# Attention with a decaying state, then a gated FFN: q's columns read as even tokens and then odd ones, and a new order for every engine

## The chip, the core and the metric

The kernel runs on one core of a Trainium2 chip. Five engines work side by side, each through its own list of instructions in order: PE (TensorE, the matmuls), ACT (ScalarE), DVE (VectorE), POOL (GpSimd) and SP (SyncE, which here only issues DMAs). The metric is the device time of one execution in microseconds. Profiles are of one execution each; times are medians of several.

## The reference

```python
f = 1.0 / (1.0 + np.exp(-f_logit))                  # q, k, v, f_logit: (4, 8, 768, 48)
for t in range(S):
    state = f[:, :, t, :, None] * state + np.einsum('bhd,bhe->bhde', k[:, :, t], v[:, :, t])
    y[:, :, t] = np.einsum('bhd,bhde->bhe', q[:, :, t], state)
x = y.transpose(0, 2, 1, 3).reshape(B * S, H * D)   # (3072, 384)
out = (np.maximum(x @ w_gate, 0.0) * (x @ w_val)) @ w_out     # d_ff 1536, float32 out
```

## The kernel before

**Attention by chunks.** Each of the four batches' 768 tokens are cut into chunks of 128. For a chunk the kernel sums the logarithms of the gates over the tokens (a matmul with a triangle), takes exponentials of the sums, scales k and q with them ("hats"), and turns both over, so that tokens lie along the columns (`qkT`). The scores of a chunk are then a matmul of the two, a mask and a matmul with v; what comes from earlier chunks is a product of q with a 48 x 48 state per head (two heads share a tile). The chunk's own k and v then bring the state forward.

**Steps and units.** The work has six steps, c = 0 to 5, each of four slots, b = 0 to 3. In steps 2 to 5 a slot is one chunk of one batch. In steps 0 and 1 two slots form a unit: a unit takes 256 neighbouring tokens of one batch, two chunks, loaded so that a partition holds a pair of neighbouring tokens. The even tokens of the pairs make one slot, the odd ones the other. A unit's keys thus lie in an order of their own, but the outputs must come out as tokens 0, 1, 2 and so on, so the score matmul reads q's columns in the order of the tokens: one column from the even tile, one from the odd tile, 64 of each, the two tiles 2 KB apart in a partition. That is `turned` (line 626); the units' scores use it (line 645) and so does their product with the state (line 703). `tmask` (lines 345 to 352) is the units' mask. Each unit's output y is copied from PSUM into `xT` (`out_way`, line 606).

**The FFN.** The 512 tokens of a step make 12 blocks of hidden columns, each of three matmuls into a gate bank (g), three into a value bank (u) (line 787), a relu on ACT or DVE (r, lines 792 and 793), and a product on DVE (p, line 795). In step 0 the first four blocks are done in two halves of 256 tokens. Then for each slot three times four matmuls with w_out (o, line 808), a copy out of PSUM (d) and a store (S).

**Names.** An operation is named by a letter, the step and the slot. L: load (f, k, q or v; the load f5.2 serves slots 2 and 3 of step 5). ef, ln: the two ACT passes over f. cum: the sum over tokens. ek, eq: exponentials. dc: decay. hk, hq: hats. tk, tq: transposes on PE (steps 0 and 1), ck, cq their copies. xh: the transposes by DMA that take their place in steps 2 to 5, on SP's queue. v: copy of v. s: scores, m: mask. y: product with v, yi: a unit's product with the state. kv, ss, sd, st: the state. x or n: copy of y; xx: the transpose by DMA into `xT` (steps 2 to 5, SP's queue). So s02 is the scores of the unit in slots 2 and 3 of step 0, g20.3 is the gate of hidden block 3 of step 2, o21.4 the second third of slot 1's output in step 2. wg, wv, wo with two numbers are loads of weights by POOL (first block + how many).

**What sets the order.** The lists `ORDER` (line 23) are written out: for each engine the operations by number, in the order in which it does them; which engine does an elementwise operation follows from the list that it stands in. A number `~25512` in PE's list stands for 25 matmuls of 512 columns on zeros (fillers, line 872), which keep PE at work. `BANKS` deals PSUM's eight banks to the operations that open one. `HELD` (line 80) makes some loads wait for the landing of another. The waits between engines follow from what an operation reads and writes. A planner outside the kernel finds the lists; it uses the costs that stand with the operations, for instance 0.01765 us for a DMA packet of a unit's load. They do nothing on the chip.

**Where an operation stands in the trace.** Engines work through their lists in order, so counting along a list gives each recorded instruction its name, and each DMA its time of landing.

## Time and profile before

| | us |
|---|---|
| runs shown | 199.95, 202.79, 202.70 |
| median | 202.7 |
| the profiled execution | 200.93 |
| its span, first to last instruction | 199.2 |
| mean granted TensorE clock | 1.000 |
| PE busy | 187.6 (94%) |
| DVE busy | 135.2 (68%) |
| ACT busy | 92.2 (46%) |
| POOL busy | 62.4 (31%) |
| HBM read and written | 25.95 and 4.72 MB |

The slices of the page cut the span into 40 equal parts of about 5 us; a digit is the busy share in tenths. The chain of waits lists in order of time what the end of the kernel hung on. In the timelines, "PE L787 ... x11 [1.53 <-DMA xT<-xn]" means eleven matmuls of that line in a row, before which PE stood idle for 1.53 us until a DMA into `xT` had landed. "SPq" is the time in which SP's queue issues a DMA: it grows when earlier transfers are not yet through.

### The profile page before, as it was taken

Reading aid. Unit: us, or ns where it says so; the run is one execution under the profiler, and the core shown is the slowest. Engines: PE = TensorE matmul, PEld = TensorE weight load, DVE = VectorE, ACT = ScalarE, POOL = GpSimd, SP = SyncE. Lnnn points to the kernel's source line nnn. Section 1 sums busy time; section 2 is a strip of 40 time slices with the busy share of each in tenths; the row PEclk is TensorE's granted clock in tenths of the full one; section 3 lists DMA queues with packets and bytes.
Section 4 is the critical chain, followed back from the end, with each engine's and each line's share of the span. In section 5 each row is a group of like instructions: output and inputs, shape, how many; then the busy total and the mean of one; then the engine's idle time right before and its main releaser. Section 6 shows DMA issues by size and latency. Waiting matters only on the chain.

```text
span 199.2 us, 4503 instructions
## 1 busy us (share of the span) xinstructions
PE 187.6 (94%) x1818; PEld 108.9 (55%) x1837; DVE 135.2 (68%) x248; ACT 92.2 (46%) x198; POOL 62.4 (31%) x93
## 2 busy tenths in 40 slices
PE   7969989999999999969999979999979999999994
PEld 2436657557565546744457644565654465455563
DVE  4179747767875979751899779687644785246841
ACT  2777744126368649831322694822166420331220
POOL 8488970041017565320612466330003000000000
PEclk9999999999999999999999999999999999999999
DMA  6999899999972999988999849996945201011103
GB/s 153 325 325 205 121 172 210 232 282 242 222 178 62 241 208 219 218 181 215 240 212 204 165 105 264 225 190 113 229 137 158 53 7 36 0 42 69 50 36 122
DMA packets 113636, 33.19 MB, mean 167 GB/s; under 512 B 106832, under 2 KB 113360, under 8 KB 113616
## 3 DMA queue, kind: packets, MB, share of 16 engines
q1 hardware_dynamic: 98432, 25.83, 57.1%
q0 software_dynamic: 3776, 3.54, 11.5%
q10 hardware_dynamic: 11408, 3.54, 7.3%
q8 instruction: 14, 0.23, 0.5%
q14 instruction: 6, 0.05, 0.1%
HBM read 25.95 MB, written 4.72 MB: 154 GB/s over the span
## 4 chain that ended last, share of the span: by engine, by line
PE 66%; DMA 10%; SPq 10%; DVE 6%; ACT 3%; ACTq 3%; issue 2%; DVEq 0%
PE ps L787 33%; PE ps L808 19%; SPq L411 6%; DMA k_in<-in_k_dram 5%; DMA f_in<-in_f_logit_dram 3%; SPq L560 3%; DVE hats L541 3%; ACTq L406 3%; PE ps L584 2%; PE ps L645 2%; PE ps L667 2%; PE ps L503 1%; PE ps L552 1%; DVE ptm L652 1%; DMA xT<-xn 1%
## 5 line engine op out<-in xcount | busy, mean ns | idle before, releaser
L795 DVE TENSOR_TENSOR gT<-relu,ps 128x512 bf16<-128x512 bf16 (+1 forms) x76 | 48.2, 656 | 21.0 <-PE ps L787 12.8
L792 ACT ACTIVATE relu<-ps 128x512 bf16<-128x512 f32 (+1 forms) x50 | 28.4, 575 | 58.7 <-PE ps L787 34.5
L787 PE MATMUL ps<-xT,wg 128*128 128x512 bf16 (+1 forms) x222 | 52.4, 368 | 2.8 <-DMA xT<-xn 2.6
L787 PE MATMUL ps<-xT,wv 128*128 128x512 bf16 (+1 forms) x218 | 52.1, 368 | 0.6
L808 PE MATMUL ps<-wo,gT 128*128 128x384 bf16 (+2 forms) x300 | 52.3, 320 | 0.0
L808 PEld LDWEIGHTS ps<-wo,gT 128*128 128x128 bf16 x300 | 27.5, 97 | 17.9 <-issue 0.5
L787 PEld LDWEIGHTS ps<-xT,wg 128*128 128x128 bf16 x228 | 23.7, 108 | 23.0 <-DMA xT<-xn 2.6
L787 PEld LDWEIGHTS ps<-xT,wv 128*128 128x128 bf16 x228 | 23.5, 108 | 18.9
L540 POOL TENSOR_TENSOR hats<-q_in,expo 128x384 bf16<-128x384 f32 x15 | 15.9, 1070 | 41.2 <-ACT expo L518 29.0
L540 POOL TENSOR_TENSOR hats<-k_in,expo 128x384 bf16<-128x384 f32 x17 | 17.5, 1036 | 16.7 <-DMA k_in<-in_k_dram 12.3
L793 DVE TENSOR_SCALAR relu<-ps 128x512 bf16<-128x512 f32 (+1 forms) x26 | 16.8, 656 | 8.3 <-PE ps L787 7.9
L592 DVE TENSOR_TENSOR ptm<-ps,tri 128x512 bf16<-128x512 f32 x32 | 20.3, 683 | 2.1 <-PE ps L584 2.1
L814 ACT ACTIVATE osb<-ps 128x384 f32<-128x384 f32 (+1 forms) x15 | 7.1, 480 | 17.7 <-PE ps L808 16.5
L456 POOL TENSOR_TENSOR st<-ssum,dec 128x384 bf16<-128x384 f32 x11 | 9.6, 880 | 16.8 <-DVE ssum L454 16.8
L478 ACT ACTIVATE f_in<-f_in 128x768 f32<-128x768 f32 x12 | 10.0, 841 | 8.4 <-issue 4.4
L516 ACT ACTIVATE expo<-ps 128x384 f32<-128x384 f32 x24 | 11.6, 495 | 1.9 <-PE ps L506 1.6
L518 ACT ACTIVATE expo<-ps 128x384 f32<-128x384 f32 x24 | 11.5, 491 | 2.3 <-DVE hats L541 1.4
L652 DVE TENSOR_TENSOR ptm<-ps,tmask 128x512 bf16<-128x512 f32 x16 | 10.3, 682 | 3.2 <-PE ps L645 3.2
L872 PE MATMUL ps<-zeros 128*128 128x512 bf16 x37 | 11.4, 452 | 0.6 <-DVE ptm L652 0.4
L481 ACT ACTIVATE bneg<-f_in 128x768 bf16<-128x768 f32 x12 | 10.0, 844 | 0.2
L815 DVE COPY osb<-ps 128x384 f32<-128x384 f32 (+1 forms) x10 | 5.3, 526 | 7.0 <-PE ps L808 7.0
L570 POOL CAST vpad<-v_in 128x384 bf16<-128x384 f32 x10 | 5.1, 518 | 15.2 <-DMA v_in<-in_v_dram 13.0
(74 smaller groups left out, 168.1 us busy)
## 6 DMA issues: line engine op xcount, KB each, us to landing
out_dram<-osb SPq DMA_DIRECT2D x23, 192.0 KB, 2.2
f_in<-in_f_logit_dram SPq DMA_DIRECT2D x11, 384.0 KB, 5.8
v_in<-in_v_dram SPq DMA_DIRECT2D x10, 384.0 KB, 6.1
q_in<-in_q_dram SPq DMA_DIRECT2D x9, 384.0 KB, 5.7
k_in<-in_k_dram SPq DMA_DIRECT2D x9, 384.0 KB, 4.8
k_in<-in_k_dram ACTq DMA_DIRECT2D x3, 384.0 KB, 7.3
q_in<-in_q_dram ACTq DMA_DIRECT2D x3, 384.0 KB, 6.0
v_in<-in_v_dram ACTq DMA_DIRECT2D x2, 384.0 KB, 6.7
```

The costliest lines, as they stand in the source:

```text
L411: op = add("L" + item, {**by("SP", lambda: sy.dma_start(dst, src), (0.42, 0.42)), **by("ACT", lambda: sc.dma_start(dst, src), (0.5, 0.5))} ...
L516: add(f"ek{c}{b}", by("ACT", lambda: sc.activation(ex[:, 1, :], bc.ap[:, 0:HD], AF.Exp, scale=1.0), act_(HD)), [bc], [f"expk{ei}"], key=P + 1)
L518: add(f"eq{c}{b}", by("ACT", lambda: sc.activation(ex[:, 0, :], bc.ap[:, 0:HD], AF.Exp, scale=-1.0), act_(HD)), [bc], [f"expq{ei}"], key=P ...
L540: return {**by("POOL", lambda: gp.tensor_tensor(o, i_, e_, ALU.mult), pool_(HD)), **by("DVE", lambda: ve.tensor_tensor(o, i_, e_, ALU.mult ...
L592: add(f"m{c}{b}{j}", by("DVE", lambda b=b, j=j, mi=mi: ve.tensor_tensor(ptm[mi][:, j, :, :], s[b, j].ap[:, :].rearrange("p (n t) -> p n t" ...
L652: add(f"m{c}{b2[i]}{j}", by("DVE", lambda i=i, j=j, mask=mask: ve.tensor_tensor(ptm[mi[i]][:, j, :, :], s[j, i].ap[:, :].rearrange("p (n t ...
L787: z = te.matmul(bank.ap[:, 0:n], wt[:, kt, w_cols(j)], xT[xi][:, kt, n0:n1], start=(kt == 0), stop=(kt == NK - 1))
L792: add(f"r{c}{b0}.{j}", {**by("ACT", lambda: sc.activation(rdst, gate.ap[:, 0:n], AF.Relu), act_(n)), **by("DVE", lambda: ve.tensor_scalar_ ...
L793: **by("DVE", lambda: ve.tensor_scalar_max(rdst, gate.ap[:, 0:n], 0.0), dve_(n))}, [gate], [f"relu{ri}"], key=P)
L795: add(f"p{c}{b0}.{j}", by("DVE", lambda: ve.tensor_tensor(gT[gi][:, j, n0:n1], rdst, val.ap[:, 0:n], ALU.mult), dve_(n)), [val, f"relu{ri} ...
L808: z = te.matmul(o.ap[:, 0:e1 - e0], gT[gi][:, j, b * C:(b + 1) * C], wo[:, j, e0:e1], start=(j == 0), stop=(j == NJ - 1))
L872: te.matmul((op.opens[0].ap if op.opens else banks[7])[:, 0:fill % 1000], zeros[:, 0:128], zeros[:, 0:fill % 1000], start=True, stop=True, ...
```

## The change

Four edits, and the lists.

1. `turned` gives the 64 even columns first, then the 64 odd ones, each in one run. The scores and the state product of the units so come out with their columns as (even, odd).
2. The masks `tmask` and `tlow` of the units are made in that order of columns: the same selections, with a pattern of two dimensions.
3. The copies x00 to x13 of the units' outputs write every other column of `xT`, so that tokens stand in order again.
4. Three costs for the planner are other numbers (loads 0.0193 and 0.0130 a packet, not 0.01765 and 0.0118; 0.64 us for a unit's product with v).
5. `ORDER`, `HELD` and `BANKS` are new. No operation is added or removed. 117 elementwise operations and loads change their engine: 38 from ACT to DVE and 28 back, 22 from POOL to DVE and 14 back, 7 loads from ACT's queue to SP's and 4 back (Lq0.2, Lv1.0, Lk2.0, Lv2.2), 4 others between ACT and POOL. Those that leave ACT's queue are Lq0.0, Lf0.2, Lq1.0, Lk1.2, Lq1.2, Lk4.2 and Lv5.0. Fillers are 42, not 40, with 22 instead of 25 at the start.

```diff
@@ masks
-            select(f"tmask{i}", tmask[i][:], -17, compare_op=ALU.is_ge, fill=0.0, base=-i, pattern=[[1, 128]], channel_multiplier=-2)
+            select(f"tmask{i}", tmask[i][:].rearrange("p (x m) -> p x m", x=2), -17, compare_op=ALU.is_ge, fill=0.0, base=-i, pattern=[[1, 2], [2, 64]], channel_multiplier=-2)
...
@@ out_way
         if X_WAY[w] == "t":
-            add(f"x{c}{b}", copies(xdst, lambda: y.ap[:, 0:HD].rearrange("p (n t) -> p n t", n=NK), HD), [y], x_key, key=P + 8)
+            xsrc = lambda: y.ap[:, 0:HD].rearrange("p (n t) -> p n t", n=NK)
+            if w < 2 * UNITS:
+
+                xdst = xdst.rearrange("p n (m i) -> p n i m", i=2)
+                xsrc = lambda: y.ap[:, 0:HD].rearrange("p (n i m) -> p n i m", n=NK, i=2)
+            add(f"x{c}{b}", copies(xdst, xsrc, HD), [y], x_key, key=P + 8)
...
@@ turned
-        return bass.AP(tensor=at.tensor, offset=at.offset, ap=[list(at.ap[0]), [1, 64], [2 * NP * C, 2]])
+        return bass.AP(tensor=at.tensor, offset=at.offset, ap=[list(at.ap[0]), [2 * NP * C, 2], [1, 64]])
```

The lists by name, cut to what the prediction speaks of (before, then after):

```
SP  before  Lf0.0 Lv0.2 Lq0.2 Lf1.0 Lk0.2 Lf1.2 Lk1.0 Lq2.2 ...
SP  after   Lf0.0 Lq0.0 Lf0.2 Lv0.2 Lk0.2 Lf1.2 Lf1.0 Lq1.2 Lq1.0 Lk1.0 Lk1.2 Lv1.2 Lf2.0 Lv2.0 Lf2.2 S00 S02
            Lq2.2 Lq2.0 Lk2.2 Lf3.0 Lq3.0 xh21 xh20 Lk3.0 xh23 xh22 S01 S03 xh31 xx20 xh30 xx21 Lv3.0 Lf3.2
            xx22 S10 xx23 Lk3.2 Lq3.2 Lv3.2 S12 S13 xx31 xh33 xh32 S11 xx30 Lq4.0 Lf4.0 Lk4.0 Lf4.2 ...
SP  before  ... Lk5.0 Lv5.2 xh42 xh43 xh51 xh50 xx41 xx40 Lk5.2 Lq5.2 Lf5.2 xx43 xx42 S32 ...
SP  after   ... Lf5.0 Lk5.0 Lk5.2 Lq5.0 xx41 xx40 Lf5.2 Lv5.0 xh51 xh50 xx42 xx43 S23 S30 Lq5.2 Lv5.2 ...
ACT before  Lf0.2 Lk0.0 Lq0.0 Lv0.0 ef00 ef02 ln00 ln02 eq01 ek01 ek00 ...
ACT after   Lv0.0 Lk0.0 Lq0.2 ef00 ln00 eq00 ek01 dc00 ek00 eq01 ef02 ck00 ln02 ck01 eq02 eq03 ek03 v02 ek02 ...
PE  before  ... cum01 cum00 cum02 cum03 ... s00 kv00 tk02 ... kv02 y00 yi01 s02 ... g00.3 u00.1 ... y02 g00.0 yi03
PE  after   ... cum00 cum01 ... tq00 ... tk00 ... tk01 kv00 ... tq01 cum02 cum03 ... s00 ... s02 y00 yi01
            cum12 cum13 u00.3 u00.2 g00.2 y02 yi03 g00.3 ...
PE  before  ... y23 cum32 kv31 kv30 cum33 o13.0 o13.4 o13.8 o11.4 o11.8 o12.8 g20.6 ...
PE  after   ... y23 s30 o13.4 o13.8 o12.0 o12.4 kv30 kv31 y31 y30 o12.8 cum32 cum33 g20.3 ...
PE  before  ... y43 o30.4 u30.10 y42 o32.4 o32.8 s50 o30.8 o33.8 o31.8 y50 g40.7 ...
PE  after   ... y43 o33.0 o33.4 u30.10 o32.0 cum53 cum52 o33.8 o30.8 o32.4 o32.8 s50 o31.4 o31.8 g40.5 ...
HELD before wg2+2 after Lq0.0, Lk1.2 after wv2+2, Lq1.0 after wv8+4, Lq2.2 after wo2+2 ...
HELD after  wo0+2 after Lv0.2, Lq1.0 after wg0+2, Lk1.0 after wg4+4, Lk1.2 after wg8+4, Lv1.0 after wo2+2 ...
```

## The prediction

> **What bounds the kernel now.** I read the rows of slices first, then the groups by shape, the chain in order of time, and the timelines of PE and of SP's queue.

> ```profile
> PE   7969989999999999969999979999979999999994
> DMA  6999899999972999988999849996945201011103
> ```

> PE is busy from end to end at a granted clock of 1.000, and until about 155 us the DMA engines are nearly as full. So a saving on PE counts, but only as far as the data keep up. A busy PE does not yet mean a fast one, so I take the pitches (start to start) from the chain, whose columns are start, length and work:

> ```profile
> 47.91 1.10 PE ps L645 x32
> ...
> 56.76 0.85 PE ps L703 x23
> ...
> 73.29 2.59 PE ps L787 x12
> 75.88 0.55 PE ps L584 x16
> ...
> 83.95 3.94 PE ps L808 x24
> ```

> A 512-column matmul of L787 takes 0.216 us, a 384-column one of L808 0.164. L645 and L584 are both eight rounds of 128 columns (four tiles a round, and two): 1.10 against 0.55 us. Only L645 reads q's columns alternately from two places 2 KB apart.

> I add up PE's list by such pitches: FFN 408 x 0.216 + 48 x 0.109 + 276 x 0.1625 + 12 x 0.109 + 12 x 0.056 = 140.2; 40 fillers x 0.216 = 8.6; the attention's matmuls 34.3; together 183.1 us. The last matmul starts at 196.4 and 2.8 us of eviction and store follow. The 13.3 us between are 7.4 lost by the start of yi03 (which stands 20.3 us into the sum and starts at 27.75), three stalls, and 1.6 in small pieces. The stalls, on PE's timeline:

> ```profile
> 89.41 2.54 PE L787 MATMUL ps<-xT,wg 128*128 128x512 bf16 x11 [1.53 <-DMA xT<-xn]
> ...
> 117.20 0.34 PE L503 MATMUL ps<-bneg,tri 128*128 128x384 bf16 x1 [1.22 <-ACT bneg L481]
> ...
> 147.83 0.60 PE L787 MATMUL ps<-xT,wg 128*128 128x512 bf16 x2 [1.07 <-DMA xT<-xn]
> ```

> Start to start, less the pitch, they are 1.70, 1.39 and 1.23: 4.3 us. The second is a load too: f4.2, issued at 108.10, lands 6.31 us later in the chain. All three end at SP's queue, which issues loads, transposes and stores in one order:

> ```profile
> 138.32 1.31 SPq L411 DMA_DIRECT2D q_in<-in_q_dram  x1
> 139.68 1.83 SPq L411 DMA_DIRECT2D f_in<-in_f_logit_dram  x1
> 141.55 4.84 SPq L611 DMA_TRANSPOSE xT<-xn  x2
> ```

> xx43 and xx42 take 4.84 us here behind three loads, against 2.55 for the pair at 135.11. A full queue passes its wait on.

> **q read in two runs.** A unit's scores have PE for 1.10 us; at L584's round, 0.55: -0.52 with the longer drain kept, four times. The inter-chunk product (L703, three rounds, 0.48) should lose 0.2, four times: -2.9 us in all. [...]

> **x copies with a 4-byte step.** Eight copies of 384 now write every other bf16; the trace has no such write. Nearest is the same copy without the step: 0.495 us on ACT into three runs, against 0.488 for xn in one run. Broken runs cost 7 ns, so I take 0. The far end is L526, whose small far-strided write takes 12 ns for four elements more, 3 ns each: +0.8 us a copy, on the path in two or three of eight, so 0 to +2; a gain is excluded, since no element is saved. [...] If instead the copies doubled as q's reading did, three on the path would add 1.5 us to the sum. The four masks keep their size (0.292 us each on POOL) and are made while PE runs fillers.

> **The start.** f0.2 moves from ACT's queue to third on SP's; ACT issues three loads first, not four. Its fourth held ACT from 4.12 to 6.40, and ef00 began at 6.45 although f0.0 had landed at 5.2. So ef00 starts about 1.2 us earlier; cum00 then waits for the 22 fillers (eleven at 0.427, eleven at 0.216 from 1.34: 8.4, against 8.99). Unit 00 comes first and its kv00 moves from 16.7 to about 13. But f0.2 lands fifth (second before), near 10, and step 0 still waits for unit 02: ef02 at 10.9, ln02 to 13.0, ek02 to 16.4, hk02 on POOL to 17.6, s02 about 20.4 (22.0 before), masks to 24.2, y02 24.3, yi03 25.3. Here it stands 18.3 us into the sum, and 162.3 follow (162.8 before). End by end: (25.3 + 162.3) - (27.75 + 162.8) = -2.95. The q saving and two more fillers (+0.4) are within it, since fillers cover s00's gain. Bounds -1.0 to -4.5: POOL puts wo0+2 and the weights wv2+2, wv0+2, wg0+2 behind sd10 and hk02, and u00.3 is late if wv2+2 lands after 23.

> **Step 1's loads.** Until now SP stood idle from 12.64 to 36.79 behind a hold. The new holds let q1.0 go when wg0+2 has landed (about 21), k1.0 after wg4+4, k1.2 after wg8+4. A load issued among POOL's weights is slow: k1.2's took 10.71 us in the chain. So q1.0 lands near 30, k1.0 and k1.2 by 36; tq10 stands at 31.0 in the sum and tk10 at 32.8, which with the 7.0 us lost by yi03 is 38 and 40. Covered, by the FFN's first hidden pieces; without them, up to 6 us. v1.0, k2.0 and v2.2 now stand on ACT behind ck13 (about 43), with d00 and v11 queued behind them. v1.0 lands about 47, kv10 is due at 43.3 + 7.0 = 50.3: covered by 2 us after its copies. f2.0 comes 8 us earlier than the 49.99 at which it landed, so cum20 (45.0 in the sum, 50.5 before) is not short. The banks are dealt anew: 0, or 0.2 us where a new tenant waits for an eviction (PE's waits for an eviction are 0.4 at most now).

> **The middle.** PE's order moves attention ahead of the FFN: s30 stands at 72.7 us of the sum (94.5 before), cum53 at 127.1 (135.4). What that does to the three stalls:
> First: between y23 and g20.3 now lie s30, y30, y31 and five pieces of o, 5.4 us of the sum (4.8 before); but xh31, xh30, Lv3.0, Lf3.2 and S10 stand among xx20 to xx23. Walking SP with its own rows (transposes 1.25 to 1.31, loads 0.5 to 1.6) from S02 at 51: xh30 lands about 79, s30 is due about 80; v3.0 lands about 83, and its copies end at 84 where kv30 is due at 83: a stall of about 1.0.
> Second: Lf4.2 starts near 100, not 108; cum43 is due at 108. Gone.
> Third: between y43 and g40.5 lie nine pieces of o, s50 and more, 7.4 us where 4.2 lay between y42 and g40.7. Gone. In its place comes f5.2. Of what stood ahead of it on SP, q5.2, v5.2, xh50, xh51 and S23 go behind (1.3 + 1.4 + 2.6 + 0.6), and k2.2, q3.0, f3.0 (0.6 + 2.6 + 2.7) are issued before xh21; back come S01 and k4.2 (2.0). So it starts at 139.7 - 9.8 + 0.7 (xh20 ends at 65.2, not 64.5) = 130.6, lands about 5 us later and its two ACT passes end near 137.5. PE would be there at 127.1 + 7.0 + 1.0 + 1.1 = 136.2: 1.3 us.
> Other changes lie beside this. DVE gets 18 more operations of 0.55 to 0.68 us, about 11 on 135 of 199. hq53 and hq52 now stand ahead of p40.1 on DVE and wait for q5.2 (about 142 to 143); eight PSUM banks let PE run some 5 us past 140. Without that cover, 1 to 2 us. At the end 53a's 256 columns are last, not 53b's 128: 0.1 us more on the copy.

> **Sum.** 199.2 - 2.95 - 4.3 + 1.0 + 1.3 + 0.1 = 194.3 us of span. Around the span lie 1.7 (the profiled execution took 200.93): 196.0. The median, 202.7, is 1.009 times the profiled execution: 197.8.

> **The rivals.** (1) SP paces it: DMA rows already full at 8 or 9 of 10 speak for that. If f5.2 starts only 6.2 us earlier (what moved behind it, with nothing won at xh21), it lands at 138, cum53 at 139.8, and 53.5 of the sum, 1.5 small pieces and 2.8 follow: 197.6, median 201.1. (2) q's reading stays at L645's pace because the weight loads hold it: the sum loses 2.4 of its gain, 196.7, median 200.2. L667, four narrower tiles in eight rounds at 0.1 us each, speaks for something between. (3) Slower: s30's transposes. xh31 and xh30 stand ahead of xx21 to xx23, each needs POOL, whose list is hq22, hq21, hk23, hq23, hk22, sd23, hq31, hq30, sd22, hk31, hk30 at 1.0 us apiece, and PE comes to s30 22 us earlier in its list. If xh30 lands when it did (91.4), s30 starts at 91.8, and 108.0 of the sum, 1 of small pieces and 2.8 follow: 203.6, median 207.1. It makes the kernel slower by 2% from a landing at 91; my walk has 79, and each of some sixteen SP entries would have to cost 0.7 more. Against it: 31 entries stand ahead of xh30, 37 before.

> **How the numbers follow.** Measurements of this kernel spread 1.4%; 2% is what can be told: 198.65 to 206.75. Forecast 0.53, own range 194 to 200; most of it, 0.46, is faster by over 2% and 0.07 within. SP's pace 0.17 and q's pace 0.10, within. s30, 0.20, slower. Range 194 (all new stalls away, 2.3 less, and 1.5 more at the start) to 207.2 (rival 3's own figure).

> **What would show it.** L645's run at about 0.55 us and L703's 0.3; x copies of 0.49 on ACT and 0.56 on DVE; y02 by 25; no wait at the g20s over 1 us, none at the g40s; xh30 landed by 80 and f5.2 by 136. A PE gap over 3 us before s30, kv30 or cum53 would make the number wrong, and so would a first FFN matmul after 26 us.

## The result and the profile after

| | before | after |
|---|---|---|
| runs | 20 | 20 |
| median | 201.88 | 201.91 |
| lowest and highest | 199.95, 204.95 | 197.75, 204.53 |
| the profiled execution | 200.93 | 199.08 |
| its span | 199.2 | 197.3 |
| mean granted TensorE clock in it | 1.000 | 1.000 |

The ratio of after to before is 0.9875, with a 95% interval of 0.9829 to 0.9921: 1.2% faster, within 2%. The ratio is taken over the executions that were not slowed, which are only five of the changed kernel's 20 (four at a mean granted clock of 0.998 or more, one at 0.991); 16 of the 20 had 0.982 to 0.991, and so the median is where it was. The experiments show that this low clock is the changed kernel's own doing.

The slices of the changed kernel, PE and DMA, look as before:

```profile
PE   7999769999999999989999999999999999999994
DMA  5999999999689693979989889797969400311004
```

What changed is in the groups by shape (busy us and mean ns of one behind the first bar). Before:

```profile
L645 PE MATMUL ps<-qkT 48*64 48x128 bf16 x128 | 4.7, 284 | 0.0
...
L597 ACT ACTIVATE xT<-ps 128x384 bf16<-128x384 f32 x6 | 2.7, 495 | 2.0 <-PE ps L667 2.0
...
L703 PE MATMUL ps<-qkT,st 128*32 128x128 bf16 x48 | 2.0, 289 | 0.0
...
L597 DVE CAST xT<-ps 128x384 bf16<-128x384 f32 x2 | 1.1, 558 | 3.0 <-PE ps L703 3.0
```

After:

```profile
L597 ACT ACTIVATE xT<-ps 128x384 bf16<-128x384 f32 x5 | 2.9, 605 | 4.0 <-PE ps L708 4.0
...
L650 PE MATMUL ps<-qkT 48*64 48x128 bf16 x128 | 2.6, 219 | 0.0
...
L597 DVE CAST xT<-ps 128x384 bf16<-128x384 f32 x3 | 1.7, 589 | 1.8 <-PE ps L672 1.8
...
L708 PE MATMUL ps<-qkT,st 128*32 128x128 bf16 x48 | 1.4, 222 | 0.0
```

Lines behind 606 are 5 further on: L650 is L645 of before, L672 was L667, L708 was L703, L792 was L787, L813 was L808. The units' scores fell from 4.7 us of busy time to 2.6 and the state product from 2.0 to 1.4. The copies into `xT` went the other way: 605 ns on ACT (495 before), 589 on DVE (558).

The timeline of PE in the changed kernel shows where the gain stayed:

```profile
22.42 0.49 PE L792 MATMUL ps<-xT,wg 128*128 128x256 bf16 x3
22.84 0.67 PE L672 MATMUL ps<-ptm,vpad 64*32 64x128 bf16 x56
26.21 0.25 PE L672 MATMUL ps<-ptm,vpad 64*32 64x128 bf16 x8 [2.71 <-issue]
26.39 0.35 PE L708 MATMUL ps<-qkT,st 128*32 128x128 bf16 x12
```

y02 is 64 matmuls that wait for nothing but what its first one has waited for. PE does 56 of them, stands for 2.71 us, and does the last 8. (The wait in brackets is the idle time just before the row.) "issue" means that no semaphore explains it. The DMA view of the stretch from 23.4 to 26.3 us (packets, MB, share of 16 engines; taken by single stretches the share can pass 100%) has one packet that is none of the kernel's:

```profile
q0 software_dynamic: 555, 0.55, 119.9%
q8 instruction: 1, 0.02, 2.0%
```

It has 16,384 bytes, runs from 24.02 to 24.97 us, and is one of fourteen along the kernel, one for some 250 recorded instructions of PE. I read it so: PE had run out of instructions, and resumes 1.2 us after the packet. Before, the same break in y02 was the chain's "26.38 0.66 issue"; it stood there already, but PE came to it later, and the packet lay at 24.35 to 25.75:

```profile
25.80 0.58 PE L667 MATMUL ps<-ptm,vpad 64*32 64x128 bf16 x45
27.04 0.35 PE L667 MATMUL ps<-ptm,vpad 64*32 64x128 bf16 x19 [0.66 <-issue]
```

Counted against the sum of PE's own pitches (183.1 us before, 180.6 after), PE has lost:

| up to the start of | before | after |
|---|---|---|
| s02 | 6.4 | 4.9 |
| yi03 | 7.4 | 8.1 |
| s20 | 8.3 | 9.8 |
| s30 | 10.0 | 10.1 |
| s32 | 10.1 | 11.6 |
| s40 | 11.9 | 13.0 |
| s52 | 13.3 | 13.9 |

The span is 1.9 us shorter: 2.5 less in the sum, 0.6 more lost. The start won 1.5 up to s02 and lost 2.2 again by yi03. Some 0.6 of that gain is this execution's luck: in the second profile of the same kernel, further down, s02 came at 19.7 and not 19.1 us, behind 11 slow fillers at the start where this one has 8. Behind yi03 the three old stalls are gone, yet the loss is 5.8 us where it was 5.9: ten waits of 0.2 to 0.9 us, counted start to start less the pitch, took their place. By the waits listed for PE, 1.1 us of what came behind 26 us hung on passes over f (bneg), 0.5 on copies of v, 0.4 on a transpose into `xT`, and 0.4 on small passes of POOL and DVE. The longest wait is cum32's, on f3.2 (0.9 us start to start, 0.75 idle by the timeline), ahead of the hidden blocks of step 2, whose own transposes are in time:

```profile
88.54 0.34 PE L503 MATMUL ps<-bneg,tri 128*128 128x384 bf16 x1 [0.75 <-ACT bneg L481]
88.81 0.32 PE L503 MATMUL ps<-bneg,tri 128*128 128x384 bf16 x1
89.08 0.81 PE L792 MATMUL ps<-xT,wg 128*128 128x512 bf16 x3
```

### The profile page after: what moved, and what is told of

Read it like the earlier page. It is cut to its first block, busy times and chain, and to the rows that moved or that the text cites. A ratio compares the mean times of both kernels' runs of the same rounds, so it can differ in the third digit from the quotient of the medians.

```text
span 197.3 us, 4513 instructions
## 1 busy us (share of the span) xinstructions
PE 187.3 (95%) x1839; PEld 107.1 (54%) x1839; DVE 143.9 (73%) x266; ACT 88.1 (45%) x190; POOL 54.7 (28%) x83
## 4 chain that ended last, share of the span: by engine, by line
PE 65%; DMA 10%; DVE 9%; ACT 7%; SPq 4%; issue 3%; POOL 1%; DVEq 0%; ACTq 0%; POOLq 0%
PE ps L792 30%; PE ps L813 20%; DMA f_in<-in_f_logit_dram 5%; PE ps L877 4%; DMA q_in<-in_q_dram 3%; DVE gT L800 2%; DMA k_in<-in_k_dram 2%; DVE hats L541 2%; PE ps L584 2%; DVE relu L798 2%; PE ps L552 2%; SPq L616 2%; SPq L560 1%; DVE ssum L454 1%; ACT expo L516 1%
## 5 line engine op out<-in xcount | busy, mean ns | idle before, releaser
L800 DVE TENSOR_TENSOR gT<-relu,ps 128x512 bf16<-128x512 bf16 (+1 forms) x76 | 48.5, 656 | 16.3 <-ACT relu L797 7.8
L792 PE MATMUL ps<-xT,wv 128*128 128x512 bf16 (+1 forms) x228 | 55.2, 368 | 0.4 <-DMA xT<-xn 0.4
L792 PE MATMUL ps<-xT,wg 128*128 128x512 bf16 (+1 forms) x228 | 55.4, 368 | 0.1
L813 PE MATMUL ps<-wo,gT 128*128 128x384 bf16 (+2 forms) x300 | 51.6, 320 | 0.0
L797 ACT ACTIVATE relu<-ps 128x512 bf16<-128x512 f32 (+1 forms) x37 | 21.7, 586 | 51.7 <-PE ps L792 31.8
L813 PEld LDWEIGHTS ps<-wo,gT 128*128 128x128 bf16 x300 | 27.4, 98 | 17.7 <-DVE gT L800 0.2
L792 PEld LDWEIGHTS ps<-xT,wv 128*128 128x128 bf16 x228 | 23.5, 108 | 19.9 <-DMA xT<-xn 0.5
L792 PEld LDWEIGHTS ps<-xT,wg 128*128 128x128 bf16 x228 | 23.4, 108 | 19.9 <-ACT expo L516 0.4
L798 DVE TENSOR_SCALAR relu<-ps 128x512 bf16<-128x512 f32 (+1 forms) x39 | 24.7, 646 | 7.4 <-PE ps L792 6.8
L540 POOL TENSOR_TENSOR hats<-q_in,expo 128x384 bf16<-128x384 f32 x13 | 13.7, 1066 | 29.8 <-DMA q_in<-in_q_dram 15.8
L540 POOL TENSOR_TENSOR hats<-k_in,expo 128x384 bf16<-128x384 f32 x13 | 13.0, 1006 | 31.1 <-ACT expo L516 29.8
L456 POOL TENSOR_TENSOR st<-ssum,dec 128x384 bf16<-128x384 f32 x12 | 10.2, 857 | 19.8 <-DVE ssum L454 19.7
L819 ACT ACTIVATE osb<-ps 128x384 f32<-128x384 f32 (+1 forms) x11 | 5.2, 482 | 21.5 <-PE ps L813 18.2
L478 ACT ACTIVATE f_in<-f_in 128x768 f32<-128x768 f32 x12 | 10.1, 839 | 8.6 <-DMA f_in<-in_f_logit_dram 8.6
L877 PE MATMUL ps<-zeros 128*128 128x512 bf16 x42 | 12.3, 430 | 0.0
L820 DVE COPY osb<-ps 128x384 f32<-128x384 f32 (+1 forms) x14 | 7.4, 534 | 6.1 <-PE ps L813 5.9
L541 DVE TENSOR_TENSOR hats<-q_in,expo 128x384 bf16<-128x384 f32 x11 | 6.6, 619 | 5.7 <-DMA q_in<-in_q_dram 3.7
L657 DVE TENSOR_TENSOR ptm<-ps,tmask 128x512 bf16<-128x512 f32 x16 | 10.1, 680 | 0.9 <-PE ps L650 0.9
L481 ACT ACTIVATE bneg<-f_in 128x768 bf16<-128x768 f32 x12 | 10.1, 840 | 0.2
```

The source lines that it names most:

```text
L456: emit = {e: (lambda g=g: g.tensor_tensor(t4(s_new), t4(tmp), rate, ALU.mult)) for e, g in (("POOL", gp), ("DVE", ve))}
L540: return {**by("POOL", lambda: gp.tensor_tensor(o, i_, e_, ALU.mult), pool_(HD)), **by("DVE", lambda: ve.tensor_tensor(o, i_, e_, ALU.mult ...
L541: **by("DVE", lambda: ve.tensor_tensor(o, i_, e_, ALU.mult), dve_(HD))}
L792: z = te.matmul(bank.ap[:, 0:n], wt[:, kt, w_cols(j)], xT[xi][:, kt, n0:n1], start=(kt == 0), stop=(kt == NK - 1))
L797: add(f"r{c}{b0}.{j}", {**by("ACT", lambda: sc.activation(rdst, gate.ap[:, 0:n], AF.Relu), act_(n)), **by("DVE", lambda: ve.tensor_scalar_ ...
L798: **by("DVE", lambda: ve.tensor_scalar_max(rdst, gate.ap[:, 0:n], 0.0), dve_(n))}, [gate], [f"relu{ri}"], key=P)
```

## The experiments

Each ratio is to the kernel before in runs on the same chip. The chips differ: the kernel before took 200.69, 203.29, 204.24 and 201.94 us (medians) beside the four sets of runs below, so only ratios and runs of one set are compared.

### The two halves of the change

The kernel before with the four edits of the code, and the changed kernel's lists with the old code:

```diff
 ORDER, HELD, BANKS of before
-ap=[list(at.ap[0]), [1, 64], [2 * NP * C, 2]]
+ap=[list(at.ap[0]), [2 * NP * C, 2], [1, 64]]
...
```

> The kernel before with the reading of q, the masks and the x copies of the change, and the old lists. Theory A (PE paces the kernel): PE's own 2.7 us of saving (scores 4 x 0.5, state product 4 x 0.17) reach the end but for s00's, which fillers cover: span about 197.0, ratio to before 0.988. Theory B (SP's queue paces it, the rival of the prediction): loads and transposes keep their times, the saving is waited out at the step 2 gate, whose 1.70 us stall grows to 3 or more; span 198.8 to 199.5, ratio 0.997 to 1.001. x copies 0.60 us on ACT as in the changed kernel, in both.

Measured: 200.78 us, ratio 0.9945 (0.9884 to 1.0006), profiled span 196.9. That lies between the two figures and decides for neither. By the timeline PE stood 1.41 us in y02, where the kernel before has 0.66 (the packet at 24.76 to 25.70), and three old stalls were there, 1.28, 0.59 and 1.19 us (1.53, 1.22 and 1.07 before).

```diff
 ORDER, HELD, BANKS of after
+ap=[list(at.ap[0]), [1, 64], [2 * NP * C, 2]]
-ap=[list(at.ap[0]), [2 * NP * C, 2], [1, 64]]
...
```

> The changed kernel's lists with the old reading of q, old masks and plain x copies. Theory A: PE's 2.7 us come back in full, span 199.8 to 200.2 and ratio 1.003 to before, that is the lists alone win nothing. Theory B: PE's extra time is covered by waits of the changed kernel (0.9 before cum32, 0.5 to 0.6 in four other places), span 197.5 to 198.6, ratio 0.99 to 0.996, that is the lists alone make most of the gain.

Measured: 204.27 us, ratio 1.0145 (1.0093 to 1.0196); both theories fell. All six runs had a clock of 0.983 or 0.991, so what the lists alone are worth at full clock is not measured, and the ratios of the two halves don't multiply to that of both. Its PE timeline has a longer stand, and its windows show what followed (the third number from the end is the granted clock, behind the busy times of the five engines). L666 here is y02's L672 of the changed kernel:

```profile
28.03 0.31 PE L666 MATMUL ps<-ptm,vpad 64*32 64x128 bf16 x8 [3.47 <-issue]
```

```profile
22.00:26.00 4.00, 2.56 (x81) 1.88 (x78) 2.72 (x6) 1.80 (x6) 1.38 (x2) 1.00 1.03 153
26.00:30.00 4.00, 1.97 (x26) 1.26 (x26) 0.93 (x2) 1.12 (x2) 0.00 (x0) 0.57 1.20 203
30.00:34.00 4.00, 4.00 (x24) 2.95 (x22) 1.43 (x5) 1.22 (x3) 0.00 (x0) 0.58 1.18 254
34.00:38.00 4.00, 3.95 (x33) 2.49 (x32) 2.54 (x6) 2.84 (x8) 2.19 (x3) 1.00 0.82 210
```

By the clock's own records it was half from 26.54 to 33.36 us, 6.83 us in all. Half the clock for 3.41 us makes a mean of 0.991 over the kernel (1 - 0.5 x 3.41 / 198), for 6.83 us 0.983: the two values that most runs of the changed kernel show. Sorted by them, its 20 runs have medians of 199.0 us (0.998 or more, four runs), 201.8 (0.991, eight) and 203.2 (0.982 or 0.983, eight).

### Whose wait is it?

The first of three edits that leave y02's data alone moves the border between two blocks of instructions: 20 of the fillers behind the first 22 are cut into 80 of 128 columns, 60 matmuls and 60 weight loads more.

```diff
-<4x512> tq00 <2x512> tk00 <3x512> tk01 ... <3x512> s02
+<16x128> tq00 <8x128> tk00 <12x128> tk01 ... <12x128> s02
```

> The changed kernel with the 20 fillers behind cum01 cut into 80 of 128 columns: the same time on PE, 120 instructions more (a matmul and its weight load each) ahead of s02. Theory I (the 2.7 us wait inside y02 is PE's instruction fetch, in blocks of about 256): the wait moves some 120 instructions towards the front, to the neighbourhood of u00.2 and g00.2 or the first matmuls of y02 at about 22.3 to 22.8 us, still 2 to 3 us long; span within 0.6 of 197.3. Rival (something that y02 needs: a mask, a bank, v): the wait stays behind matmul 56 of y02's 64.

Measured: 198.35 us, ratio 0.986 (0.9804 to 0.9916), three of four runs at a clock of 1.000. The stand left y02 and came into a row of matmuls of one hidden block, which wait for nothing either (timeline of PE):

```profile
22.06 0.72 PE L792 MATMUL ps<-xT,wv 128*128 128x256 bf16 x5
24.12 0.27 PE L792 MATMUL ps<-xT,wv 128*128 128x256 bf16 x1 [1.34 <-issue]
```

So the place is set by the count of instructions: PE resumes behind 703 to 705 recorded instructions here, in both kernels and in the other versions whose stand lies in this stretch. Theory I had the place; the stand was shorter than the 2 to 3 us it had expected (1.34), and the span, 195.8, was 1.5 below that of the changed kernel, where I had the same within 0.6. The second edit thins out the DMAs at that time:

```diff
-POOL ... wg4+4 wv4+4 wg8+4 wv8+4 hq12 hq10 hq11 ...
+POOL ... hq12 wg4+4 wv4+4 wg8+4 wv8+4 hq10 hq11 ...
```

> The changed kernel with hq12 ahead of the four large weight loads on POOL, so that they are issued from about 23.5 us and not from 18.6. Theory I with contention (the block of instructions waits behind POOL's transfers): the block is fetched by 22, the wait in y02 falls under 0.7 us, first FFN blocks of hidden 4 and later wait at most 0.5; span 194.8 to 196, ratio 0.977 to 0.985. Theory I without contention (a fetch always takes its 4 to 6 us): the wait stays at 2.5 to 3 and the span at 197 to 198. If the weights are late, PE waits before g00.5 or u00.6 near 30.

Measured: 200.35 us, ratio 0.9967 (0.992 to 1.0015). The packet came 1.7 us behind the border, not 4.0 (no trace marks the border; I estimate it at some 250 recorded instructions ahead of the place where PE resumes, as there is one packet for some 250, which puts it at 20.0 us in the changed kernel), and the stand in y02 fell to 0.59 us by the timeline:

```profile
24.01 0.67 PE L668 MATMUL ps<-ptm,vpad 64*32 64x128 bf16 x56
25.27 0.25 PE L668 MATMUL ps<-ptm,vpad 64*32 64x128 bf16 x8 [0.59 <-issue]
```

From 22 to 26 us the DMAs moved 100 GB/s on average, against 161 in the changed kernel. But between the border and the packet, the time in which a load on the DMAs would hold it up if the transfer is asked for at the border, which is not shown, the rate was 135 GB/s here and 138 in the changed kernel; so the packet came earlier, and why it did is not shown. The gain did not last, and the ratio expected, 0.977 to 0.985, was missed: y10 stood 2.25 us at 53.9 for a later such packet, and smaller waits followed.

A third edit puts more work between the border and the stand (g00.1, u00.0 and g00.0 come forward too):

```diff
-u00.3 u00.2 g00.2 y02 yi03 g00.3 u00.1 g02.2
+u00.3 u00.2 g00.2 g00.3 u00.1 y02 yi03 g00.1 u00.0 g00.0 g02.2
```

> The changed kernel with the PE order of the first step altered: the hidden tiles g00.3 and u00.1 (two groups of 3 matmuls of 256 columns, 0.33 us each) come ahead of y02 instead of behind yi03, with r00.3, p00.3, r00.1 and p00.1 moved along on DVE; nothing is added or left out. Theory I (TensorE waits for its next 16 KB of instructions, whose transfer began at 24.02 us and ended at 24.96 in the changed kernel, whatever TensorE does meanwhile): the wait stays in y02, but TensorE has 0.65 us more work ahead of it, so it falls from 2.7 us to 1.7-2.4 us; with a shorter wait fewer runs lose granted clock: under half of them below 0.995 (16 of 20 in the changed kernel); median 200.0 us. Rival C (the wait is set by how TensorE's instructions run, and shifts with them): 2.7 us again, clock below 0.995 in most runs, median 202.

Measured: 202.18 us, ratio 0.9903 (0.9861 to 0.9945). The stand was 1.88 us by the timeline against 2.71 in the changed kernel, as theory I has it, though the packet, at 24.84, was also 0.8 us later than there and PE reached the place 1.6 us later; but 7 of 12 runs were below 0.995, where it had expected under half. What half the clock does is seen in the groups of three behind the stand, 0.50 us in the changed kernel (lines of this experiment are 58 less):

```profile
27.02 0.30 PE L614 MATMUL ps<-ptm,vpad 64*32 64x128 bf16 x14 [1.88 <-issue]
27.25 0.51 PE L650 MATMUL ps<-qkT,st 128*32 128x128 bf16 x12
27.69 0.82 PE L734 MATMUL ps<-xT,wg 128*128 128x256 bf16 x3
28.31 0.85 PE L734 MATMUL ps<-xT,wv 128*128 128x256 bf16 x3
```

### Does a stand alone take the clock down?

```diff
-HELD = {56: 48, 60: 69, 62: 54, 65: 57, 68: 64, 71: 59, 376: 71}
+HELD = {56: 48, 60: 69, 62: 54, 65: 57, 68: 64, 71: 59, 376: 71, 138: 246}
```

> The kernel before with one wait added: y02 on TensorE waits for hk11 on POOL, which ended at 28.52 us there; y02 was ready at 25.8. So TensorE stands for about 2.7 us at the place where the changed kernel stands for its instructions, with nothing else changed; the instructions will have come by then. Theory K (a stand of this length makes the chip grant half the clock for one or two windows of 3.41 us in most runs, whatever its cause): mean granted clock 0.982-0.991 in most runs, median 204.0 (200.7 + 2.1 for the wait less what was waited there already + 1.2 to 3.4 for the clock). Rival D (the low clock of the changed kernel has another cause: its denser start, or the transfer itself): clock 0.999 or more in nearly all runs, as in the kernel before, median 202.5.

138 is y02, 246 is hk11. Measured: 206.07 us, ratio 1.0136 (1.0083 to 1.019); all six runs had a clock of 0.982 to 0.992, while 13 of the 17 runs of the kernel before beside them had 0.999 or more. Theory K holds. The median is 2 us above the 204.0 expected, and where the rest lies was not followed. The timeline and the windows of its profile:

```profile
28.40 0.73 PE L667 MATMUL ps<-ptm,vpad 64*32 64x128 bf16 x64 [2.89 <-POOL hats L540]
```

```profile
26.00:30.00 4.00, 1.60 (x80) 1.08 (x81) 0.00 (x0) 0.92 (x3) 2.25 (x4) 0.96 1.21 190
30.00:34.00 4.00, 4.00 (x27) 3.00 (x24) 2.64 (x7) 1.15 (x3) 0.00 (x0) 0.61 1.16 210
34.00:38.00 4.00, 3.95 (x32) 2.86 (x32) 2.53 (x8) 1.29 (x3) 0.00 (x0) 1.00 1.08 233
```

### The copies with a step

This version leaves out the order of the tokens, even ones first, in steps 0 and 1: its copies write runs of elements, without the step of two, but its results are not those wanted.

```diff
-            if w < 2 * UNITS:
-                xdst = xdst.rearrange("p n (m i) -> p n i m", i=2)
-                xsrc = lambda: y.ap[:, 0:HD].rearrange("p (n i m) -> p n i m", n=NK, i=2)
```

> The changed kernel with the x copies of steps 0 and 1 written straight, without the 4-byte step that restores the order of tokens: the output rows of steps 0 and 1 lie in the order even, odd within a chunk, that is, the reordering is left out. Theory S (the step makes the copies dearer): ACT's x copies of 128x384 go from 605 back to 495 ns, DVE's from 589 to 558; on the path that is at most 0.3 us, so the median stays within 0.5 us of the changed kernel's. Rival T (the copies are dearer for what they collide with at that time, not for the step): 590 ns or more on ACT still.

Measured: 199.68 us, ratio 0.9845 (0.9787 to 0.9902), the changed kernel's within the intervals. Three of its four runs kept a clock of 1.000, although PE stood 2.59 us in y02 in its profile: a stand there does not cost the clock each time. In the groups by shape:

```profile
L597 ACT ACTIVATE xT<-ps 128x384 bf16<-128x384 f32 x5 | 2.3, 489 | 4.9 <-PE ps L704 3.8 <-PE ps L668 1.1
L597 DVE CAST xT<-ps 128x384 bf16<-128x384 f32 x3 | 1.6, 551 | 1.6 <-PE ps L668 1.6
```

With the step the same rows have 605 and 589 ns. Theory S: the step costs ACT 0.12 us a copy and DVE 0.04.

### What is late at the start of step 2

```diff
-SP ... S01 S03 xh31 xx20 xh30 xx21 Lv3.0 Lf3.2 xx22 ...
+SP ... S01 S03 Lf3.2 xh31 xx20 xh30 xx21 Lv3.0 xx22 ...
```

> The changed kernel with 20 fillers cut to 128 columns as in the experiment before (198.35 us there), and on SP the load f3.2 moved from behind v3.0 to right behind S03, where SP's queue stood idle for 3.2 us (71.74 to 74.94 in the changed kernel). Theory F (the first stall of step 2 is the wait of cum32 for f3.2, which was issued at 81.7 and landed at 86.7 because SP was busy without a pause from 74.9 on): the stall at 87 us (0.9 us in the changed kernel, 1.73 in the kernel with short fillers) falls below 0.4, and xx22, xx23, k3.2, q3.2 and v3.2 are issued up to 1.7 us earlier; span 194.2, median 197.0, ratio to before 0.978-0.983. Rival N (what is late next takes its place, as after the three stalls that the change removed): a stall of over 0.8 us within 10 us behind 87, median 198.0-198.6, ratio 0.985-0.99.

Measured: 199.97 us, ratio 0.9831 (0.9784 to 0.9879). The time is above what F and N had expected, and the ratio at the edge of F's. Five of six runs had a lowered clock (0.983 or 0.991), with 1.8 us of stand at 22.9, in the row in which the first version with short fillers had 1.34 us and one lowered run of four: the same fillers are cut in both, so the shifted border alone does not keep the clock. N was right about the place: cum32's wait was gone, and PE stood for v3.0 in its stead (L714 is kv's line, L767 of before; waits of PE from 80 to 95 us: total, times, longest).

```profile
PE ps L714 <- ACT vpad L514: 1.2, 1, 1.2
```

So both loads were put into the idle time, and 17 fillers cut, not 20 (the last three are left whole):

```diff
-SP ... S01 S03 xh31 xx20 xh30 xx21 Lv3.0 Lf3.2 xx22 ...
+SP ... S01 S03 Lf3.2 Lv3.0 xh31 xx20 xh30 xx21 xx22 ...
```

> The changed kernel with 17 fillers cut into 68 of 128 columns (the border of TensorE's instruction blocks moves 102 instructions ahead), and both f3.2 and v3.0 on SP issued right behind S03, in the idle time that f3.2 alone filled in the run before, where v3.0 became late (landed at 88.4) and kv30 waited 1.49 us at 87.7. Theory F2 (with both loads early nothing is late at the start of step 2): no wait over 0.6 us on TensorE between 80 and 95 us; against the run with f3.2 alone (ratio 0.983) 1.0 to 1.5 us less, ratio to before 0.975-0.980. Rival N (xx21, xx22 or the next SP item is late in its place): a wait of 0.8 us or more there again, ratio 0.982-0.987. The instruction wait at 22-24 us is 1.3 to 2.1 us by both, and the clock below 0.995 in up to half of the runs.

Measured: 198.42 us against 204.24, ratio 0.973 (0.9672 to 0.9788), all six runs at a clock of 1.000; theory F2 had 0.975 to 0.980. PE waits for nothing listed between 80 and 95 us, and its stand at the border of blocks is short:

```profile
23.53 0.24 PE L614 MATMUL ps<-ptm,vpad 64*32 64x128 bf16 x5
24.87 0.69 PE L614 MATMUL ps<-ptm,vpad 64*32 64x128 bf16 x59 [1.11 <-issue]
```

The next late loads showed elsewhere: PE stood 1.49 us before cum41 at 109.1 (0.26 in the changed kernel) and 1.02 before kv12 at 52.1. This version beats both kernels: on the same chip the changed kernel gave this:

> The changed kernel as it is, beside the two above on the same chip. By theory K (a stand of 2.7 us, with the short ones behind it, costs one or two windows at half the clock in most runs) its clock is 0.982 to 0.992 in over half of the runs and its median 1 to 2 us above that of its undisturbed runs, ratio of all its runs to before near 0.995 and of the runs at full clock 0.985-0.990; by rival D (the low clock belonged to the chips of the first measurement) the clock is 0.998 or more in nearly all runs.

Measured: 202.58 us, ratio 0.986 (0.9791 to 0.9929); four of six runs between 0.982 and 0.991, and in y02 a stand of 2.58 us by the timeline. Theory K again. It lies 4.2 us above the version with both loads early in median.

That version with the order g00.3 u00.1 y02 of the earlier experiment:

> As the run with both loads early and 17 fillers cut, with the PE order of the run that put g00.3 and u00.1 ahead of y02 as well. Theory I (the instruction wait shrinks by what work is put into the block): the wait at 22-25 us is 0.6 us shorter than without this order (0.7 to 1.5 us), and the clock is 0.995 or more in over 8 of 10 runs; ratio 0.970-0.977. Rival C (the wait shifts along): 1.3 to 2.1 us again, clock as without, ratio the same as without or up to 0.3 us worse for the later x02.

Measured: 198.66 us, ratio 0.9725 (0.9673 to 0.9776), five of six runs at 0.999 or more. Nothing gained over the run without that order. In the profiled execution the stand was 2.29 us, in u00.1, as the packet itself took 2.73 us, not 0.94, from 22.45 on; that one can't tell theory I from C.

Which of the two edits brought the 0.973? The loads alone:

```diff
 PE ... <4x512> tq00 <2x512> tk00 <3x512> tk01 ...
-SP ... S01 S03 xh31 xx20 xh30 xx21 Lv3.0 Lf3.2 xx22 ...
+SP ... S01 S03 Lf3.2 Lv3.0 xh31 xx20 xh30 xx21 xx22 ...
```

> The changed kernel with f3.2 and v3.0 issued right behind S03 on SP and its fillers as they are: the run of both (ratio to before 0.973, clock 1.000 in 6 of 6) without the shift of the instruction blocks. Theory K (the low clock comes from the 2.7 us instruction wait, which stays here): the wait in y02 is 2.5 to 2.8 us, mean clock 0.982 to 0.992 in over half of the runs, ratio of the undisturbed runs 0.978-0.983, median of all runs 1.5 to 3 us over the one of both. Rival L (the early loads brought all of it): clock 0.999 or more in most runs and ratio 0.971-0.975.

Measured: 200.82 us against 201.94, ratio 0.9874 (0.98 to 0.9947), 3.1 us of stand in y02, and five of six runs at 0.983 or 0.991. The sixth, at 0.999, took 197.56, 0.978 of the median before. So theory K: the loads help, but without the shifted border the clock takes most of it back. The ratio expected of runs at full clock, 0.978 to 0.983, is borne out by that one run alone. The border alone gave 0.986, the loads alone 0.9874, both 0.973, with an interval apart from those of either: it takes both.

## Why the prediction was right and where it was wrong

The likeliest case was 197.8 us and over 2% faster; it came out at 201.91, within the range of 194.0 to 207.2 and within 2%, the case with a chance of 0.34. That it lies there is no credit to what was named for that case: the supply of instructions and the clock, which no rival named, held it there. Where the clock was full the forecast was near: 197.8 predicted, 199.0 the median of four executions. In the profiled execution the span was to be 194.3 and was 197.3: 1.1 us of that at the start, 1.9 behind it.

**q read in two runs: right.** A unit's scores take 0.64 us with the drain where 1.17 stood by the timeline, start to start 0.57 where 1.10 stood, 2.1 less in four runs, and the state product 0.7 less: 2.9, the figure predicted (two more fillers leave 2.5 of it in PE's sum). The rival that the weight loads hold q at its old pace is out.

**x copies: a small size missed.** 0 was taken, 0.11 us a copy on ACT and 0.03 on DVE were measured, and the copies without the step are at 489 and 551 ns, against 605 and 589 with it. At most 0.3 us of it can lie on the path.

**The start: the step that failed.** yi03 was to begin at 25.3, 2.45 us earlier than before, and began at 26.39, 1.36 earlier. The walk of data was even too careful: y02 began at 22.84, not 24.3, and without the stand yi03 would have begun at 23.7, not 25.3. The sum let PE go as soon as data and banks were there. Instructions have to be there too: a block of them lasts PE only 3.2 to 4.8 us in this stretch by its pitches, while the packet began 4.0 us behind the border and was of use 2.2 us later. The 0.66 of "issue" in the chain before was a sign of it, and was passed over.

**Step 1's loads: right.** q1.0 landed at 33.3, 3 us later than forecast and still in time, k1.0 at 35.3, k1.2 at 36.5, v1.0 at 48.5; tq10 came at 39.5, kv10 at 52.0.

**The stalls: named ones right, the rest not.** The second and third went. The first stayed at 0.9 (1.0 predicted), but on f3.2 at cum32, not on v3.0 at kv30; when f3.2 was moved, v3.0 was late, so the two were within a microsecond. f5.2 was issued at 134.2, not 130.6, and landed at 137.8; cum53 came at 140.7 and waited for nothing, so 1.3 us fell away. Where the sum failed is the 1.6 us for small pieces: 5.8 us were lost behind yi03, 3.9 predicted. Where PE comes earlier it meets what is next late, a load, a copy or a transpose as listed above; only two such were priced. That each of the ten waits goes back to a load was not followed.

**The median: wrong in its factor.** 1.009 times the profiled execution was taken over from before; it was 1.014, because the clock was down in most executions (16 of 20 at 0.982 to 0.991), as it was in all six runs of the kernel before with an added stand (2.89 us in the profiled one).

**The rivals.** SP's pace had a median of 201.1 close to the one measured, but not its mechanism: f5.2 held nothing up. s30's transposes landed at 81.9 (xh30), not at 91, and s30 began at 82.7. Two signs of being right were missed by some 2 us without harm: xh30 was to land by 80, f5.2 by 136.

## What to carry to other kernels

A wait of PE in the middle of a row of equal matmuls, marked "issue", is worth looking up among the transfers of instructions: where many small matmuls follow one another, as y02's 64 did here with 2.71 us of stand among them, the supply of instructions belongs into the sum beside data and banks. A stall that is taken away is worth what the next late operand leaves of it (three stalls of 4.3 us went here, and the loss behind yi03 fell from 5.9 to 5.8 us), so price the next two or three as well. And compare the granted clock of all runs, not of the profiled one alone: a profile at 1.000 stood for 4 of 20 executions here.

## What the runs showed of the hardware

**Instructions come in blocks and can be late.** The packets have 16,384 bytes; PE resumed 1.2 to 1.5 us after the end of one, where it stood for it. Between PE's passing the border before, as estimated above, and the start of the packet lay 1.7 us with the weights put later, and 2.2 to 4.6 in other profiles (3.0 before, 4.0 in the changed kernel, 2.2 in the run with the added wait, which has the DMAs of before). What makes it late stays open: the spread is nearly as wide without a change of the DMAs, and the rate between border and packet, 135 GB/s against 138, does not tell the early one from the late. Most of the packets come without a stand of PE (thirteen of fourteen in the changed kernel's profile); the one in this stretch comes with one, of 0.6 to 3.5 us, in every profile but that of the run with the added wait.

**The first fillers.** Between 7 and 14 of the first fillers took 0.427 us instead of 0.216, in kernels whose first instructions are alike (10 before, 8 after and 11 in the second profile of the same kernel, 14 with the weights later). In the kernels with the changed lists the first matmul behind the fillers began between 7.61 and 9.04 us, 1.4 us apart.
